# An adaLN transformer block on one core: feed-forward units of 1, 1, 2, 4, 4, 4 tiles, feature-major first keys, and a new order of loads and instructions

## The chip, the core and the metric

The kernel runs on one core of a Trainium2 chip. A core has engines that run side by side, each with its own in-order queue: TensorE (PE in the profile, its weight loads PEld), VectorE (DVE), ScalarE (ACT), GpSimd (POOL) and SyncE (SP), which here issues nearly all DMA transfers. Matmuls write to PSUM, which the kernel divides into a double bank for the attention sums (`kv_ps`) and six single banks (`one_ps`). The metric is the device time of one execution in microseconds (us), the median over runs.

## What is computed

One block with adaptive layer norm, over S = 2048 tokens of width D = 512, all in bf16:

```python
mod = (silu(c) @ w_mod)           # sa, ca, ga, sb, cb, gb: six rows of 512
h = layernorm(x) * (1 + ca) + sa
x = x + ga * A(h)
h = layernorm(x) * (1 + cb) + sb
x = x + gb * B(h)
```

```python
# A: linear attention, 32 heads of 16
q, k, v = h @ wqkv
pq, pk = q @ w_phi, k @ w_phi     # one 16 x 16 matrix per head
phi = [softmax(p), softmax(-p)]   # over 16 features, for q and for k
o = (phi_q @ (phi_k^T v)) / (phi_q @ sum(phi_k) + 1e-6)
return o @ wo
# B: feed-forward, F = 1376
return (silu(h @ w_gate) * (h @ w_up)) @ w_down
```

## The kernel before, in words

Tokens are cut into 16 tiles of 128, four tiles to a chunk (`x_ch`, 512 tokens each). Every step of the block is written as an operation of a planner (`pl.op`) with the buffers that it reads and writes, its estimated cost, and sometimes a choice of engines. `ORDER` (lines 46 to 87) is a long list, written out by hand or by a search, of operation numbers and engine choices. `Plan.run` walks through it, gives each operation a start time from its cost table, hands out the slots of the rotating buffers, and emits all operations by that start time. What each engine executes, and in which sequence, is thus fixed at build time; on the chip semaphores only make it wait. Where the planned start times leave PE idle, `fill` (line 1012) puts in matmuls on a tile of ones (line 1029), whose result is never used.

The work has these stages.

1. Loads (lines 428 to 438), all on SP's queue in order of their planned times: `x` of chunk 0, `wk`, `wphi`, the first third of `w_mod` in two pieces, `x` of chunk 1 in two pieces with `wq` between, `wv`, `x` of chunks 2 and 3. Later weights are queued further on.
2. Modulation columns. `silu(c)` (lines 445 to 457), then `mod_cols` (line 462): matmuls of the `w_mod` columns with it (line 468), copied out as `modA` (shift and 1 + scale) by two DVE instructions.
3. Folding. `w_phi` is spread into a block-diagonal matrix `BD` (lines 489 to 500). `fold_phi` (line 504) multiplies it into `wk` and `wq`: turn the weight (on PE for `wk`, by DMA transpose for `wq`), copy it out (`WT`, line 519), multiply by `BD` (line 526), write it back over the weight (line 529). So `pk = h @ Wk2` takes one matmul chain.
4. First norm (`first_norm`): `bn_stats` per tile on DVE (line 345), `rstd`, then the normalized tile `xn`. `turn_tile` (line 553) turns the first four tiles on PE into one bank each, and ACT or DVE evacuate it in two halves as `hT`, feature-major, with the modulation applied (lines 565 and 567). Later tiles go through `modulate_T` or a DMA transpose.
5. Keys and values (`k_tile`, line 615): four matmuls of 512 columns for `pk` (line 622), two exps on ACT into `e` (line 633), four matmuls for `v` (line 626), sums over 16 features on DVE (`S`, line 639), reciprocals, the weighted `va` (line 649), POOL's multiply (line 656). `kv_tile` adds a tile's `phi_k^T [v, 1]` into `kv_ps` (line 662). When all 16 are in, DVE masks the sum into `KVZ` (lines 771, 773).
6. Queries (`q_tile`): the same with `wq` into a tile `eq` of its own for each of the 16 tiles, `Sq` on DVE (line 693), then a DMA transpose into `pT` (line 704).
7. Attention of a tile (`attend_tile`): eight matmuls (line 805), a reciprocal `A`, the division into `o` (line 809). `turn` turns `o` into `oT`, on PE for the first two tiles and by DMA on SP (line 828) after that. `project` multiplies by `wo` (line 838), adds to `x` on DVE (line 841), and does the second norm. `second_T` turns that and applies `modB`.
8. Feed-forward in units of `UNITS` (line 33): `(chunk, first tile, tiles)`. `prepare` does stage 7 for the tiles of a unit, one or two at a time. `ffn_tail` does the last 96 of the 1376 hidden features, `ffn_gu` (line 878) the others in groups that fill a bank of 512: with w tiles, 4 / w blocks of 128 features, so that one matmul has 128 w columns (line 890). ACT takes silu of the gate bank (line 897); the product with the up bank is made by DVE (line 900), or for every other group by ACT's copy and POOL (lines 904, 906). `ffn_down` (line 946) accumulates 11 matmuls of 512 columns for each tile (line 962), scales, adds and stores (line 982).

Of the kernel before, what the change touches and what calls it, by code (L numbers as in the profile page):

```python
# [7 lines left out]
BF16 = mybir.dt.bfloat16  # L8
FP32 = mybir.dt.float32
ACT = mybir.ActivationFunctionType  # L10
ALU = mybir.AluOpType
# [21 lines left out]
UNITS = [(0, 0, 1), (0, 1, 1), (0, 2, 1), (0, 3, 1), (1, 0, 2), (1, 2, 2), (2, 0, 2), (2, 2, 2), (3, 0, 2), (3, 2, 2)]  # L33


def fm_size(m):
# [10 lines left out]
    0, 4, 8, 44, 64, 48, 52, 132, 116, 12, 56, 68, 76, 72, 172, 80, 164, 136, 176, 16, 60, 148, 100, 120, 168, 196, 200, 124, 85, 152, 180, 140,  # L47
    156, 88, 105, 92, 184, 108, 204, 190, 208, 128, 98, 216, 20, 240, 161, 228, 212, 264, 144, 225, 194, 112, 220, 420, 272, 244, 268, 32, 276, 24,
    28, 233, 248, 312, 36, 252, 236, 257, 376, 548, 281, 364, 512, 424, 284, 260, 428, 320, 432, 40, 294, 400, 552, 516, 324, 316, 588, 290, 480,
    592, 329, 296, 304, 472, 301, 380, 332, 524, 308, 596, 437, 338, 388, 520, 384, 444, 368, 372, 464, 456, 484, 440, 416, 529, 852, 556, 342, 404,  # L50
    476, 756, 448, 452, 532, 460, 856, 392, 408, 584, 468, 560, 344, 544, 488, 492, 510, 536, 396, 800, 760, 764, 502, 498, 541, 412, 600, 565, 572,
    1064, 506, 628, 1068, 808, 816, 1072, 624, 932, 768, 568, 605, 608, 984, 724, 632, 988, 820, 576, 636, 358, 860, 928, 350, 361, 792, 692, 732,
    354, 728, 773, 892, 804, 956, 1312, 812, 580, 796, 960, 824, 700, 848, 964, 1316, 612, 780, 896, 620, 828, 616, 864, 776, 784, 845, 788, 869,
    640, 968, 833, 972, 992, 888, 842, 938, 1000, 1280, 952, 976, 996, 946, 949, 904, 900, 876, 660, 1004, 942, 909, 872, 980, 838, 1160, 884, 881,
    916, 1276, 912, 1240, 920, 696, 1009, 1164, 1244, 736, 1324, 1028, 1168, 1016, 1304, 924, 1172, 1021, 1196, 1012, 1200, 1328, 1024, 740, 1294,
    1177, 644, 1252, 744, 1184, 1336, 1289, 1236, 1180, 1076, 1208, 1297, 1248, 648, 1257, 1264, 1189, 1204, 1332, 1341, 1286, 1492, 1496, 1192,
    1212, 748, 664, 1269, 1217, 1320, 1260, 1344, 1532, 1348, 1272, 1572, 1500, 1612, 1576, 1504, 1396, 1356, 1224, 1300, 1220, 1584, 1080, 652,
    1536, 1232, 1540, 1509, 1229, 1360, 668, 656, 1589, 1544, 1516, 1616, 1512, 1352, 1549, 1528, 1521, 1568, 1580, 1524, 1624, 1556, 1620, 1596,
    1592, 1629, 1561, 1601, 1604, 1636, 1641, 1552, 1608, 1084, 1564, 1632, 1128, 1136, 1716, 1644, 1648, 1796, 1800, 1780, 704, 1804, 1088, 1808,
    1652, 1748, 1724, 672, 1828, 1784, 1788, 1832, 1836, 1132, 1720, 752, 1792, 1404, 1400, 1408, 1756, 1308, 1684, 1032, 1092, 1840, 1660, 1844,  # L60
    2288, 2292, 1428, 1848, 708, 2296, 2300, 1036, 676, 1040, 1852, 1856, 2452, 1688, 712, 1860, 716, 720, 1752, 680, 1044, 1096, 684, 1864, 1436,
    1432, 1460, 1104, 1692, 1656, 1364, 1869, 2456, 2304, 1872, 1100, 1048, 1880, 1052, 2460, 2136, 2308, 1877, 1884, 1948, 688, 1056, 2312, 2140,
    1944, 1368, 1468, 1060, 1464, 2316, 1924, 1372, 2144, 1108, 1412, 1928, 1888, 1112, 1908, 2440, 1936, 1912, 2320, 1916, 1140, 2444, 2326, 1116,
    1120, 2148, 2152, 1416, 2328, 1144, 2448, 1892, 1932, 1920, 1984, 1124, 1940, 1952, 1148, 1896, 2338, 2156, 1988, 2334, 1960, 1900, 1964, 2160,
    2164, 1152, 1992, 2345, 2168, 1956, 1376, 2464, 1472, 2341, 2400, 2348, 2404, 1996, 2174, 2692, 1904, 1156, 2352, 2408, 2176, 2696, 1420, 1380,
    1384, 1476, 2384, 2700, 2000, 1388, 2392, 2492, 2496, 2181, 1968, 2356, 2004, 1480, 2704, 2468, 2193, 2190, 1424, 2364, 2008, 2186, 2380, 2412,
    2248, 2012, 2708, 2368, 2372, 1392, 2016, 2388, 2472, 2500, 2712, 2020, 2360, 2396, 2025, 1972, 2216, 2256, 2036, 2040, 2028, 2956, 2716, 2196,
    2376, 2476, 1484, 2960, 2504, 2252, 1488, 2964, 2228, 2508, 2032, 2236, 2260, 2480, 2484, 2513, 2490, 2516, 2044, 2048, 2944, 1440, 2096, 2416,
    2100, 2948, 1444, 1448, 1452, 1664, 2200, 2420, 1668, 1672, 1676, 2104, 2424, 2744, 2052, 2720, 2952, 1456, 3208, 2108, 2748, 2204, 2533, 2752,
    2232, 2525, 2530, 2724, 2756, 2212, 2968, 2240, 1680, 2522, 3212, 2760, 2728, 3216, 2076, 2220, 2732, 2736, 2536, 2742, 2540, 1696, 2224, 3196,  # L70
    2208, 2608, 2765, 1700, 2084, 3200, 1760, 2996, 2972, 2616, 2428, 3204, 1704, 1708, 1764, 2244, 2544, 2060, 1728, 2768, 1768, 2548, 2064, 3448,
    2080, 2068, 1772, 2782, 1712, 2773, 2556, 2778, 2576, 3220, 1732, 2785, 3000, 3452, 1776, 2976, 1736, 3456, 2628, 2788, 2792, 2088, 1740, 1744,
    3460, 2072, 2980, 2984, 2264, 2092, 3004, 2584, 3464, 3248, 2988, 3008, 3468, 2993, 3224, 2268, 3252, 3012, 3228, 3712, 3472, 3716, 3017, 2636,
    2272, 3232, 3236, 2612, 2796, 3720, 2560, 3256, 3240, 2800, 3020, 3260, 3700, 3264, 2564, 3704, 1976, 2056, 2112, 3476, 3708, 3480, 2620, 3026,
    3500, 2632, 3245, 3504, 3508, 3724, 3033, 3037, 2116, 3030, 2624, 3040, 2276, 3512, 3516, 3044, 2120, 3269, 3484, 3272, 3132, 2592, 2640, 2572,
    3488, 3492, 3521, 3498, 2568, 2124, 3752, 2596, 2600, 3140, 2552, 3756, 2580, 2804, 3285, 3278, 1980, 3760, 3524, 2588, 2604, 3728, 1824, 3281,
    3289, 3732, 2280, 3048, 3292, 3736, 3296, 3300, 3537, 3764, 2668, 3530, 3542, 2672, 3740, 3768, 3533, 3744, 2676, 2828, 3544, 3304, 3749, 3052,
    2836, 3548, 3774, 3776, 2680, 2685, 2644, 2648, 2880, 2888, 2652, 2884, 2848, 2656, 2892, 2688, 3790, 3782, 3056, 2844, 3785, 2824, 2864, 3793,
    2852, 3796, 2432, 2436, 2832, 2808, 2128, 2856, 3800, 2816, 2812, 2820, 2860, 3816, 3804, 2840, 2920, 3808, 2896, 2132, 2872, 3308, 2868, 2876,
    2900, 2904, 3824, 2924, 2928, 3820, 2932, 2908, 3832, 3836, 3840, 3828, 3844, 3076, 3552, 2937, 3080, 3084, 3136, 3848, 3088, 2940, 3928, 3092,  # L80
    3852, 3144, 3860, 3872, 3812, 3868, 3876, 3096, 3856, 3100, 3864, 3880, 3884, 3060, 1812, 2284, 2660, 3932, 3104, 3888, 3896, 3064, 3556, 3892,
    3116, 3108, 3068, 3124, 2912, 3112, 3120, 3072, 3900, 3936, 3128, 3172, 3312, 3148, 3176, 3180, 3184, 3152, 3320, 3156, 3904, 2916, 3316, 3908,
    3332, 3912, 3940, 3945, 3948, 3328, 3189, 3324, 2664, 3340, 3560, 3336, 3916, 3364, 3368, 3921, 3384, 1817, 3160, 3372, 3344, 3376, 3380, 3392,
    3348, 3352, 3388, 3356, 3360, 1821, 3400, 3404, 3396, 3408, 3424, 3192, 3428, 3432, 3616, 3436, 3600, 3441, 3624, 3924, 3564, 3620, 3165, 3584,
    3444, 3636, 3628, 3592, 3168, 3580, 3568, 3412, 3640, 3572, 3588, 3632, 3576, 3416, 3644, 3608, 3596, 3604, 3648, 3676, 3612, 3652, 3680, 3420,
    3684, 3656, 3688, 3660, 3952, 3664, 3692, 3956, 3696, 3960, 3669, 3964, 3672, 3968,
# [35 lines left out]
class Plan:  # L122


    HOP = {"PE": 0.24, "DVE": 0.2, "ACT": 0.2, "POOL": 0.14, "SP": 0.0, "XBAR": 0.08, "NONE": 0.0}
    OWN = {"PE": 0.0, "DVE": 0.19, "ACT": 0.19, "POOL": 0.12, "SP": 0.0, "XBAR": 0.0, "NONE": 0.0}
    DMA = (1.7, 385e3, 0.5, 0.7, 1.3, 1.0)
# [81 lines left out]
def kernel(  # L209
# [23 lines left out]
    wts = ctx.enter_context(tc.tile_pool(name="wts", bufs=1))  # L233
    attn = ctx.enter_context(tc.tile_pool(name="attn", bufs=1))
    lnp = ctx.enter_context(tc.tile_pool(name="lnp", bufs=1))
    ps = ctx.enter_context(tc.tile_pool(name="ps", bufs=1, space=PSUM))

    slots = {"raw": 2, "st6": 6, "one": 6, "four": 1, "xn": 4, "raw1": 2, "nmr": 4, "ln2": 6, "xn2": 2, "WT": 2, "e": 6, "S": 3, "R": 3,
             "va": 6, "Sq": 4, "Rq": 4, "pT": 4, "A": 2, "o": 2, "oT": 2, "sg": 3, "gu": 13, "gul": 3, "sgl": 3,
             "usb": 2, "ot": 3, "fg": 3}  # L240
    pl = Plan(slots)
    pools = {}

    fixed = {}

# [185 lines left out]
    for k in (0, 2):  # L431
        later(wmod_sb[:, k:k + 2, 0:2 * D], wmod_v[:, k:k + 2, 0:2 * D], bm1[k:k + 2], 512)
# [636 lines left out]
```

The softmax here doesn't subtract the row's maximum and nothing guards it: scores larger than these inputs give would overflow.

## Time and profile before

| | us |
|---|---|
| median of 3 runs | 201.79 |
| span of the profiled execution, first to last instruction | 200.1 |
| PE busy (matmuls x1743) | 192.4 (96%) |
| PE weight loads busy (x1765) | 131.7 (66%) |
| DVE busy | 136.7 (68%) |
| ACT busy | 111.4 (56%) |
| POOL busy | 124.4 (62%) |
| share of the chain that ended last on PE | 85% |
| gate and up matmuls (line 890, x800), busy | 75.4 |
| down matmuls (line 962, x167 and 11 of the last half tile), busy | 39.6 and 1.4 |
| DMA moved | 24.22 MB, mean 121 GB/s |

How to read it: the span is one execution under the profiler; the median is taken over runs that include what lies around the span. The page's slices cut the span into 40 pieces of 5 us and give tenths of busy time. A table of stages gives the busy microseconds of each engine and the number of its instructions. The chain of waits goes back from the last instruction to what released it each time, so that its pieces lie one after the other in time. In the timeline, an instruction is followed by the idle time before it and what ended that. Matmul records overlap, since one starts before the one ahead has drained; the time from start to start is what one more matmul costs.

### The profile page before, as it was taken

To read this page: it belongs to the slowest core of one execution; us is meant where nothing else is said; L and a number is where in the kernel's file an instruction comes from. 1 tells how busy PE (TensorE), PEld (TensorE's weight loads), DVE (VectorE), ACT (ScalarE), POOL (GpSimd) and SP (SyncE) were. 2 spreads that over 40 slices of the span, in tenths; PEclk is the share of its full clock that TensorE was granted. 3 is DMA by queue.
4 is the path that set the end of the run, shared out by engine and by line. 5 is a ranking of instruction groups with operands and counts; after the bars stand their busy time and mean duration, and the time that the engine had idled before them with its cause. 6 is when DMAs were issued, how large, how long until landed. Compare 5 with 4: busy or idle time off the path is not lost.

```text
span 200.1 us, 4635 instructions
## 1 busy us (share of the span) xinstructions
PE 192.4 (96%) x1743; PEld 131.7 (66%) x1765; DVE 136.7 (68%) x274; ACT 111.4 (56%) x249; POOL 124.4 (62%) x209
## 2 busy tenths in 40 slices
PE   7898999999999989999999999999999999999993
PEld 2654546454554867896796676688488865867852
DVE  5898999999899989998997896432041404434143
ACT  2689999989779963572554717344154230421510
POOL 3445999999998697687896689744123920210602
PEclk9999999999999999999999999999999999999999
DMA  6998998991963694956695463042010001101102
GB/s 212 342 316 193 278 244 238 227 358 25 216 209 76 131 130 95 114 108 124 113 194 105 64 131 79 3 92 66 3 56 10 5 26 52 52 3 41 36 6 66
DMA packets 51081, 24.22 MB, mean 121 GB/s; under 512 B 42257, under 2 KB 47858, under 8 KB 51058
## 3 DMA queue, kind: packets, MB, share of 16 engines
q1 hardware_dynamic: 50912, 23.85, 50.8%
q8 instruction: 14, 0.23, 0.5%
q14 instruction: 9, 0.07, 0.1%
q10 hardware_dynamic: 146, 0.07, 0.1%
HBM read 11.58 MB, written 2.10 MB: 68 GB/s over the span
## 4 chain that ended last, share of the span: by engine, by line
PE 85%; ACT 5%; DVE 5%; DMA 2%; issue 1%; DVEq 0%; SPq 0%; ACTq 0%
PE one_ps L890 33%; PE one_ps L962 19%; PE one_ps L626 7%; PE one_ps L838 6%; PE one_ps L685 5%; PE one_ps L622 5%; PE one_ps L930 3%; DVE st L345 2%; PE kv_ps L662 2%; DMA oT<-o 2%; ACT e L633 2%; PE kv_ps L805 2%; ACT hT L565 1%; ACT eq L689 1%; PE kv_ps L1029 1%
## 5 line engine op out<-in xcount | busy, mean ns | idle before, releaser
L890 PE MATMUL one_ps<-hT,wgu_sb 128*128 128x256 bf16 (+1 forms) x800 | 75.4, 251 | 0.0
L890 PEld LDWEIGHTS <-wgu_sb 128*128 128x128 bf16 x800 | 65.3, 98 | 9.4
L906 POOL TENSOR_TENSOR gu<-usb,sg 128x512 bf16<-128x512 bf16 x16 | 18.5, 1157 | 38.1 <-ACT usb L904 18.8
L897 ACT ACTIVATE sg<-one_ps 128x512 bf16<-128x512 f32 (+1 forms) x42 | 23.5, 576 | 32.1 <-PE one_ps L890 27.8
L962 PE MATMUL one_ps<-wd_sb,gu 128*128 128x512 bf16 (+3 forms) x167 | 39.6, 372 | 0.5
L900 DVE TENSOR_TENSOR gu<-one_ps,sg 128x512 bf16<-128x512 f32 (+1 forms) x26 | 16.6, 643 | 24.4 <-PE one_ps L890 20.2
L962 PEld LDWEIGHTS <-gu 128*128 128x128 bf16 (+1 forms) x187 | 17.9, 98 | 15.9
L973 DVE TENSOR_TENSOR fg<-one_ps,gab 128x512 bf16<-128x512 f32 (+1 forms) x16 | 10.5, 668 | 24.2 <-PE one_ps L962 23.4
L345 DVE BATCH_NORM_STATS2 st<-x_c 128x6 f32<-128x512 bf16 x32 | 21.3, 676 | 0.1
L639 DVE TENSOR_REDUCE S<-e 128x64 f32<-128x1024 bf16 x16 | 19.2, 1203 | 0.7 <-issue 0.5
L693 DVE TENSOR_REDUCE Sq<-eq 128x64 f32<-128x1024 bf16 x16 | 19.0, 1192 | 0.0
L700 POOL TENSOR_TENSOR eq<-eq,Rq 128x512 bf16<-128x512 bf16 x16 | 16.9, 1056 | 0.8
L689 ACT ACTIVATE eq<-one_ps 128x512 bf16<-128x512 f32 x32 | 17.1, 613 | 0.4 <-PE one_ps L685 0.3
L633 ACT ACTIVATE e<-one_ps 128x512 bf16<-128x512 f32 x32 | 16.8, 605 | 0.8 <-PE one_ps L622 0.6
L904 ACT CAST usb<-one_ps 128x512 bf16<-128x512 f32 x16 | 9.3, 583 | 14.2 <-PE one_ps L890 13.0
L656 POOL TENSOR_TENSOR e<-e,S 128x512 bf16<-128x512 bf16 x16 | 16.8, 1057 | 0.3
L626 PE MATMUL one_ps<-wv,hT 128*128 128x512 bf16 x61 | 15.7, 378 | 0.8 <-ACT e L633 0.6
L838 PE MATMUL one_ps<-wo_sb,oT 128*128 128x512 bf16 x60 | 15.6, 379 | 0.9 <-DMA oT<-o 0.7
L622 PE MATMUL one_ps<-wk,hT 128*128 128x512 bf16 x62 | 15.7, 379 | 0.1
L685 PE MATMUL one_ps<-wq,hT 128*128 128x512 bf16 x61 | 15.1, 379 | 0.1
L841 DVE TENSOR_TENSOR x_c<-x_c,one_ps 128x512 bf16<-128x512 bf16 x16 | 10.8, 674 | 6.0 <-PE one_ps L838 6.0
L393 ACT ACTIVATE xn<-x_c,ln_nmr,ln_rstd 128x512 bf16<-128x512 bf16 x10 | 8.1, 809 | 9.7 <-POOL ln_nmr L359 9.7
(112 smaller groups left out, 268.2 us busy)
## 6 DMA issues: line engine op xcount, KB each, us to landing
wmod_sb<-in_w_mod_dram SPq DMA_DIRECT2D x2, 1024.0 KB, 7.0
out_dram<-ot SPq DMA_DIRECT2D x15, 128.0 KB, 1.9
x_c<-in_A_x_dram SPq DMA_DIRECT2D x3, 512.0 KB, 4.1
wgu_sb<-in_B_w_gate_dram SPq DMA_DIRECT2D x1, 1376.0 KB, 6.8
wgu_sb<-in_B_w_up_dram SPq DMA_DIRECT2D x1, 1376.0 KB, 6.7
wd_sb<-in_B_w_down_dram SPq DMA_DIRECT2D x1, 1280.0 KB, 7.4
wmod_sb<-in_w_mod_dram SPq DMA_DIRECT2D x2, 512.0 KB, 6.4
wk<-in_A_wqkv_dram SPq DMA_DIRECT2D x1, 512.0 KB, 4.7
```

Source lines behind the costliest of these rows:

```text
L345: pl.op("DVE", r=reads, w=[st6], us=0.6, fn=lambda: nc.vector.bn_stats(st6()[:], src))
L622: nc.tensor.matmul(pk()[:], lhsT=hT[c_i][k][:, cols], rhs=Wk2[:, k, :], start=(k == 0), stop=(k == KD - 1))
L626: nc.tensor.matmul(v()[:], lhsT=hT[c_i][k][:, cols], rhs=wv_sb[:, k, :], start=(k == 0), stop=(k == KD - 1))
L633: nc.scalar.activation(e()[:, :, sg].rearrange("p g h f -> p g (h f)"), pk()[:].rearrange("p (g n) -> p g n", g=G), ACT.Exp, scale=(1.0, - ...
L639: pl.op("DVE", r=[e], w=[Ss], us=1.14, fn=lambda: nc.vector.tensor_reduce(Ss()[:].rearrange("p g s h -> p (g s h)"), e()[:].rearrange("p g ...
L685: nc.tensor.matmul(pq()[:], lhsT=hT[c_i][k][:, cols], rhs=Wq2[:, k, :], start=(k == 0), stop=(k == KD - 1))
L689: pl.op("ACT", r=[pq, btab], w=[be[sg]], us=0.48, fn=lambda sg=sg: nc.scalar.activation(eq[:, :, sg].rearrange("p g h f -> p g (h f)"), pq ...
L693: pl.op("DVE", r=be, w=[Sq], us=1.14, fn=lambda: nc.vector.tensor_reduce(Sq()[:].rearrange("p g s h -> p (g s h)"), eq[:].rearrange("p g s ...
L838: nc.tensor.matmul(a()[:], lhsT=oT()[:, j0 + j, :], rhs=wo_sb[:, j, :], start=(j == 0), stop=(j == KD - 1))
L890: nc.tensor.matmul(ps_()[0:fsz, q * n:(q + 1) * n], lhsT=wgu_sb[:, k, i, m * P:m * P + fsz], rhs=h2[k], start=(k == 0), stop=(k == KD - 1))
L897: pl.op("ACT", r=[g, btab], w=[sg], us=0.08 + 0.41 * L / CW, fn=lambda: nc.scalar.activation(sg()[0:fsz, 0:L], g()[0:fsz, 0:L], ACT.Silu))
L962: nc.tensor.matmul(fp()[:], lhsT=b()[0:fsz, c0:c0 + P], rhs=wd_[0:fsz, m, wcs], start=(m == 0), stop=(m == FM - 1))
```

## The change

Six things change together.

- `UNITS` becomes one unit of one tile, another, one of two, and three of four, instead of four of one tile and six of two. A unit of four still prepares two tiles at a time. `ffn_tail` works on two tiles at a time in a buffer of its own (`gut`), and `gu` has 20 slots instead of 13.
- The keys of tiles 0 and 1 no longer wait for the folded weight: `first_keys` multiplies the plain `wk` with `hT` of both tiles, 256 columns wide, into feature-major keys `kT`, and `k_tile` multiplies those by `BD`. `kT` lies in the memory of the last tile's `eq`. Folding `wk` goes on as before, now after these reads.
- `turn_tile` turns each half of a tile into a bank of its own.
- `mod_cols` lets a one-row matmul write the zeros and ones first, so that one copy takes out `modA` or `modB`.
- The first loads are cut and listed anew.
- The planner's costs are changed throughout, and `ORDER` is a new list.

Only costs, that is estimates of the planner, change in the places that are not shown.

```diff
-UNITS = [(0, 0, 1), (0, 1, 1), (0, 2, 1), (0, 3, 1), (1, 0, 2), (1, 2, 2), (2, 0, 2), (2, 2, 2), (3, 0, 2), (3, 2, 2)]
+UNITS = [(0, 0, 1), (0, 1, 1), (0, 2, 2), (1, 0, 4), (2, 0, 4), (3, 0, 4)]
...
-             "va": 6, "Sq": 4, "Rq": 4, "pT": 4, "A": 2, "o": 2, "oT": 2, "sg": 3, "gu": 13, "gul": 3, "sgl": 3,
+             "va": 6, "Sq": 4, "Rq": 4, "pT": 4, "A": 2, "o": 2, "oT": 2, "sg": 3, "gu": 20, "gut": 5, "gul": 3, "sgl": 3,
...
-    later(x_ch[0][:], x_v[0], bx[0:4], 512)
-    later(Wk2[:], wqkv_v[:, :, D:2 * D], bwk[0:1], 560)
-    later(wphi_sb[:], A_w_phi.rearrange("h (q t) f -> (h q) (t f)", t=4), [bphi], 80)
-    for k in (0, 2):
-        later(wmod_sb[:, k:k + 2, 0:2 * D], wmod_v[:, k:k + 2, 0:2 * D], bm1[k:k + 2], 512)
-    later(x_ch[1][:, 0:2, :], x_v[1][:, 0:2, :], bx[4:6], 256)
-    later(x_ch[1][:, 2:4, :], x_v[1][:, 2:4, :], bx[6:8], 256)
+    later(x_ch[0][:, 0:2, :], x_v[0][:, 0:2, :], bx[0:2], 230)
+    for k, n, kb in ((0, 2, 660), (2, 1, 300), (3, 1, 300)):
+        later(wmod_sb[:, k:k + n, 0:2 * D], wmod_v[:, k:k + n, 0:2 * D], bm1[k:k + n], kb)
+    later(Wk2[:], wqkv_v[:, :, D:2 * D], bwk, 560)
+    later(wphi_sb[:], A_w_phi.rearrange("h (q t) f -> (h q) (t f)", t=4), [bphi], 100)
+    later(x_ch[0][:, 2:4, :], x_v[0][:, 2:4, :], bx[2:4], 270)
+    for t in (0, 2):
+        later(x_ch[1][:, t:t + 2, :], x_v[1][:, t:t + 2, :], bx[TPC + t:TPC + t + 2], 270)
...
         def fm(k):
+            if k == 0:
+                nc.tensor.matmul(mp()[:, 0:8], lhsT=ones[0:1, 0:P], rhs=zero_one[0:1, :], start=True, stop=False, skip_group_check=True)
...
         def fc():
-            nc.vector.tensor_copy(mt[:, 0:KD], mp()[:, 0:KD])
-            nc.vector.tensor_scalar_add(mt[:, KD:2 * KD], mp()[:, KD:2 * KD], 1.0)
+            nc.vector.tensor_copy(mt[:], mp()[:])
...
     def turn_tile(xn, parts, q, t):
-        tp = bank("T", [P, KD, P], BF16)
...
         for jp in range(2):
+            tp = bank("T", [P, 2, P], BF16)
+
+            def ft(jp=jp, tp=tp):
+                for jj in range(2):
+                    j = 2 * jp + jj
+                    nc.tensor.transpose(tp()[:, jj, :], xn()[:, q, j * P:(j + 1) * P], ident_b[:])
...
+    kT = eqs[NT - 1][:].rearrange("p g s h f -> p (g s h f)").rearrange("p (j m) -> p j m", j=KD)
+    bkT = [Buf(), Buf()]
+
+    def first_keys():
+        for jp in range(2):
+            pp = bank("kv", (P, 2, 2 * P))
+
+            def f(k, jp=jp, pp=pp):
+                for jj in range(2):
+                    j = 2 * jp + jj
+                    nc.tensor.matmul(pp()[:, jj, :], lhsT=Wk2[:, k, j * P:(j + 1) * P], rhs=hT[0][k][:, 0:2 * P],
+                                     start=(k == 0 and jj == 0), stop=(k == KD - 1), skip_group_check=True)
+            for k0 in (0, 2):
+                pl.op("PE", r=[bhT[0][t][k] for t in (0, 1) for k in (k0, k0 + 1)] + bwk[k0:k0 + 2], w=[pp], us=0.44,
+                      fn=lambda f=f, k0=k0: (f(k0), f(k0 + 1)))
+            pl.op([("ACT", 0.48, lambda jp=jp, pp=pp: nc.scalar.copy(kT[:, 2 * jp:2 * jp + 2, :], pp()[:])),
+                   ("DVE", 0.6, lambda jp=jp, pp=pp: nc.vector.tensor_copy(kT[:, 2 * jp:2 * jp + 2, :], pp()[:]))],
+                  r=[pp], w=[bkT[jp]])
...
+        def fk2():
+            for j in range(KD):
+                nc.tensor.matmul(pk()[:, j * P:(j + 1) * P], lhsT=kT[:, j, cols], rhs=BD[:, j].rearrange("p h f -> p (h f)"),
+                                 start=True, stop=True)
...
-        pl.op("PE", r=h_bufs(i) + bWk2, w=[pk], us=0.865, fn=fk)
+        if i < 2:
+            pl.op("PE", r=bkT + [bBD], w=[pk], us=0.23, fn=fk2)
+        else:
+            pl.op("PE", r=h_bufs(i) + bWk2, w=[pk], us=0.865, fn=fk)
...
     first_norm(0, 2)
+    bmodA = mod_cols(modA, 0, [[b] for b in bm1])
+    first_T(0, 2)
+    first_keys()
     fold_phi(D, Wk2, bWk2, bwk)
     first_norm(2, 2)
-    bmodA = mod_cols(modA, 0, [[b] for b in bm1])
-    first_T(0, 2)
...
     def ffn_tail(unit, guT):
...
+        g = min(w, 2)
+        guT[FM - 1] = []
+        for p0 in range(0, w, g):
+            gu = sb("qf", "gut", [P, 2 * P], BF16)
+            ps_ = bank("gu")
```

In the built program, SP issues the first transfers in this sequence: `x` of chunk 0 in two halves, `x` of chunk 1 in two halves, `w_mod` in three pieces, `wphi`, `wk`, `x` of chunk 2, `wv`, `wq`. PE does the first key matmuls between the turns of `wk`, and none of the filler matmuls stands after them (before, five stood between the last `kv_tile` and the second norm of tile 0). DVE has the eight `bn_stats` of chunks 0 and 1 ahead of its copy of `modA`.

## The prediction

> **What bounds the kernel now.** I read the 40 slices first, then the busy time by stage, then the chain of waits, then the timeline of the start and of 57 to 74 us.
>
> ```profile
> PE   7898999999999989999999999999999999999993
> DVE  5898999999899989998997896432041404434143
> ```
>
> TensorE (PE) is busy from the second slice to the last, VectorE (DVE) up to the 24th. By stage (us, then busy us of PE, weight loads, DVE, ACT, POOL):
>
> ```profile
> 0.00:11.70 11.70, 9.61 (x112) 5.66 (x114) 8.19 (x28) 6.21 (x14) 4.82 (x18) 1.00 0.87 292
> 11.70:18.00 6.30, 5.71 (x40) 3.06 (x39) 6.15 (x18) 5.67 (x14) 3.40 (x6) 1.00 1.09 231
> 18.00:57.30 39.30, 38.93 (x324) 20.86 (x330) 38.11 (x61) 36.80 (x102) 37.16 (x62) 1.00 0.87 233
> 120.00:197.00 77.00, 76.61 (x578) 56.53 (x582) 26.19 (x48) 26.35 (x49) 29.89 (x34) 1.00 0.12 34
> ```
>
> From 18 to 57 us all four engines are full; after 120 us PE alone. Busy time flatters PE, so I count necessary work: matmuls in the program times the start-to-start time that the chain shows.
>
> ```profile
> 48.56 0.86 PE one_ps L685 x4
> ...
> 81.76 4.02 PE one_ps L890 x72
> ...
> 182.29 8.74 PE one_ps L890 x80
> ```
>
> 512 columns take 0.216 us (four in 0.86), 256 take 0.109 (8.74 / 80), 128 take 0.056 (4.02 / 72). So 429 x 0.216 + 502 x 0.109 + 408 x 0.056 + 64 of 192 columns x 0.083 + 256 of 68 columns x 0.031 + 84 small x 0.025 = 185.4 us without the fillers of line 1029. What PE lacks is clock time minus necessary work issued: 8.0 us at the first keys (11.72 us, 3.7 done), 9.0 at 18 us, 9.3 at the first attention matmul (57.30), 10.2 at the first gate/up (66.56), 11.3 at the first down (73.78), 11.4 at PE's end (196.83). Behind that lie 3.3 us of last add and store. So the time is 185.4 + 11.4 + 3.3 = 200.1, and only the 9.0 of the start and the 2.4 gained between 18 and 74 us can shrink. Of the 2.4 the largest is this:
>
> ```profile
> 68.31 3.96 DMA oT<-o
> 72.32 0.39 PE one_ps L838
> ```
>
> The transpose of o is issued late (SP stood behind three pT transposes from 62.51) and the projection waits for it.
>
> **What the Trainium skill says.** "TensorE: Matmul & The Clock Gate", Back-to-back issue gap: columns / 2.4 + 2.5 ns, so larger matmuls save only the 2.5. The trace agrees (216, 109, 56 ns). "Perfetto Trace Analysis", Identifying the Most-Contended Engine: judge TensorE by weight-load share. Here that is 66% and 98 ns per load, yet starts keep column pace even at 256 columns, so I give nothing for fewer loads. Same page, Matmuls: groups should rotate through banks so evacuation overlaps; the trace agrees, ACT's hT waits 0.6 for DVE's hT on a shared bank. "PSUM — Partial Sum Buffer", Engine vs sequencer instructions: ACT and DVE queues are strict first-in-first-out; the start's working rests on it.
>
> **The change, part by part.**
>
> *Units.* 160 matmuls of 128 and 400 of 256 columns go, 240 of 512 come: 160 x 0.056 + 400 x 0.109 = 52.6 against 51.8, **-0.8**. Evacuations stay 512 wide; three up halves move from DVE to ACT and POOL (3 x 0.58, 3 x 1.16), hidden after 120 us, where each is busy a third. SP issues three transposes fewer. The two zero_one matmuls cost 0.05 of PE, under waits for wmod; one modA instruction less saves 0.1 of DVE, in the start below. Were that cover gone, each would count in full, a tenth of a microsecond.
>
> *Keys from unfolded weights.* Eight 512-column matmuls go (1.73), 16 of 256 (1.75) and 8 of 128 (0.45) come: **+0.5**. The 256-column form with hT moving is not in the trace; I take the gate/up row of that width (0.109), between 0.107 (columns alone) and 0.126 (two of 128 columns and a start each). ACT gets two copies of kT (0.98). kT lies in the tile eq15, whose own exp comes some 40 us later: no wait. PE's work is 185.1 in all.
>
> *First loads.* Landings before: wk 5.88 (issue 1.18 + 4.7), the wmod halves 8.09 and 9.55, wq 11.68 (3.68 + 8.0), wv 13.89 (4.79 + 9.1). So 512 KB take 1.46, and the small w_phi 0.75 (8.09 - 5.88 - 1.46). In the built program SP's order is x 0 and x 1 in four halves, wmod in three, w_phi, wk, x 2, wv, wq: landings 3.7, 4.4, 5.15, 5.9; 7.3, 8.1, 8.8; 9.55; 11.0; 12.5; 13.9; 15.4. The key weights come 5 us later, x 1 over 4 us earlier, wv as before. The ninth load waits for the first to land, long before its turn. Queued behind on SP are x 3 and the four wq transposes: they slip from 11.8 to about 16, and the first fold of wq, at 16.8 before, is placed after 14.6 us of PE work, about 24: no wait.
>
> *The start, by queues.* DVE gets x at 3.75; eight bn_stats (0.595 each), aggregates (0.09) and the silu steps (0.65) all stand before its modA copy: 9.9 (10.14 before). Then ACT evacuates hT at 0.70 a pair: the first two end 11.4, and the first key matmul starts there, with 2.4 us of work done: 9.0 lacking, against 8.0. ACT goes on in order: hT 12.1, two WT copies (0.48) 13.0, hT 13.7, kT 14.2 and 14.7, wk 15.2, 15.7, 16.15. PE meanwhile does 16 key matmuls, weight turns and folds, v of one tile (wv 13.9), and the two BD products when banks come free (16.0, 16.6: the second after DVE's wk copy, which stands behind four bn_stats of x 2). The first exp starts about 16.4 against 13.99, tile 2's keys at 16.8 with 7.2 done: 9.6 lacking against 9.0: **+0.6**. What is queued behind the second BD product on PE, tile 2's keys, needs the same copy, so that wait is paid once. Bounds: -0.5 (PE without a gap from wk's landing: 11.0 with 1.9 done lacks 9.1, and 8.5 if the loads land 0.6 sooner) and +1.6 (ACT's hT pairs at the 0.81 of a lone pair and another bank late). From there banks (73, 75, 74) come free just as PE asks.
>
> *18 to 74 us.* DVE's work up to KVZ grows by 1.8 (one Sq 1.13, one WT copy 0.36, two hT 0.58, less small ones) but its idle time falls from 4.85 (by stages up to KVZ, 55.81) to about 2.3, as x comes early: KVZ at 55.1, PE there at 56.3. No wait. After that the built order does more projections before the first gate/up (58.0 of work done, 56.3 before), so tile 0's chain has 6 us instead of 4.6, and no filler stands after the first keys (five did at 55 to 66, 0.85 us). The oT for the next two projections: o done 63, one pT ahead on SP, +3.2 to landing: 66.3, PE at 66.6. I take 0.75 of waits in place of 2.4 (0.2 at the first turn, which stands behind an Sq on DVE; 0.35 up to KVZ as before; 0.2 for the projections): **-1.65**. What is late next would be VectorE. Bounds: 0 and 4 (rivals 1 and 2).
>
> *End.* Same last add and store: 3.3.
>
> Sum: -0.3 + 0.6 - 1.65 = -1.35 from the span of 200.1; runs lie 1.7 above the span (median 201.79), so **200.4**.
>
> **The rivals.**
> 1. *No wait after 18 us:* the order leaves no room. PE lacks 9.6 at the end: -0.3 - 1.8 = 199.7; with the start 0.5 better than by my queues (the exact landing of x decides), 199.2. For it: after 74 us the kernel before loses 0.1. Against: 18 to 57 us is full on four engines.
> 2. *VectorE late, slower:* DVE becomes the bound. If its idle before KVZ is 1.2 above my 2.3 (e's come 2.4 later from ACT), attention waits us for us; the u halves and projections that DVE must free hold up to six banks at 75 to 90 us, since two more Sq's, one more o and one more x + A stand before the first gate/up multiply. Idle as before (4.85) gives KVZ 57.6, 1.4 late; the same again in the banks: 200.4 + 2.8 = 203.2. Against: 23 to 24 slices of DVE at 8 to 9 left PE no gap before.
> 3. *The oT wait stays:* SP's pT waits for POOL's eq as at 62.51 (5.18 for three); 1.1 comes back: 201.5. And the change doesn't do what it says: keys start no earlier by my working, which is already in the sum.
>
> **How the numbers follow.** Forecast 0.52 (199.6 to 201.2), rival 1 0.22, rival 2 0.16, rival 3 0.10. The range drops the outer parts of rivals 1 and 2: 198.6 to 203.3. Two per cent, about what a measurement of this kernel can tell from no change, is 197.75 and 205.8. Below needs PE to lack 7.7, when wk alone lands at 11.0 with 2 us done: only if loads run faster than 512 KB in 1.2, 0.1. Above needs rival 2 doubled: 0.09.
>
> **What would show it.** Right: first key matmul near 11.4, first exp near 16.4, KVZ near 55, gate/up 216 ns apart, weight loads near 50%, PE ending near 195.5. Wrong: keys before 10.5 (landings), DVE idle over 4 us before KVZ, or ACT and DVE groups waiting on banks between 75 and 120 us.

## The result, and the profile after

The changed kernel takes 202.12 us (median of 7, 201.56 to 205.57) against 201.69 for the kernel before on the same chip: ratio 1.0027, interval 1.0010 to 1.0043. It is 0.4 us longer, not 1.4 shorter. The profiled execution has a span of 200.1 us, the same as before. Some executions of the changed kernel lose about 2 us, a few more than 3, to a granted clock that falls to half (for 3.4 us in the profiles that show it); where I give a mean span below, it is over executions with a granted clock of 0.997 or more (here 200.1 in 6 of 7; 199.8 for the kernel before, taken beside the experiments), and the ratios leave the longest executions out.

The slices and the busy times of the profiled execution:

```profile
PE 193.4 (97%) x1463; PEld 108.3 (54%) x1463; DVE 141.1 (70%) x285; ACT 107.6 (54%) x242; POOL 123.7 (62%) x202
...
PE   7699999999999999999999999999999999999993
...
DVE  6899999998999999979997946446405202314443
```

The weight loads fell from 66% to 54% as forecast, and PE looks full. Two rows of the table of stages (us, then busy us of PE, weight loads, DVE, ACT, POOL) show where it is not:

```profile
0.00:11.70 11.70, 8.65 (x88) 4.46 (x89) 8.87 (x35) 5.42 (x11) 4.25 (x18) 1.00 0.83 283
...
118.00:137.00 19.00, 18.44 (x95) 8.42 (x93) 10.46 (x22) 9.85 (x18) 10.66 (x17) 1.00 0.27 54
```

PE was busy 9.61 us of the first stage before; in the second row, a stretch for which the prediction has no term, 0.56 us is missing. What PE lacks, counted as in the prediction (clock time minus necessary work issued) but from start to start for both kernels, is:

| PE lacks, us | before | after |
|---|---|---|
| at the first key matmul | 7.9 (11.72) | 9.7 (12.18) |
| at tile 2's keys (before: 18 us) | 8.9 | 9.7 (17.04) |
| at the first attention matmul | 9.1 (57.30) | 10.1 (57.08) |
| at the first gate/up | 10.0 (66.56) | 10.3 (68.46) |
| at the first down | 11.1 (73.78) | 10.3 (76.58) |
| at PE's end | 11.2 (196.83) | 11.4 (196.82) |

Read down, the kernel before loses 2.2 between 18 and 74 us and 0.15 after that. The changed kernel loses 0.6 up to its first down matmul, and then 1.1. The gain of the middle is there, and 0.95 of it is given back later. The timeline of PE at that place (start, us, engine, line, tiles, count, idle time before):

```profile
127.59 1.03 PE L926 MATMUL one_ps<-hT,wgu_sb 128*128 128x512 bf16 x4
128.90 3.63 PE L926 MATMUL one_ps<-hT,wgu_sb 128*128 128x512 bf16 x16 [0.28 <-DVE hT L895]
...
133.56 1.89 PE L926 MATMUL one_ps<-hT,wgu_sb 128*128 128x512 bf16 x8
135.73 1.02 PE L926 MATMUL one_ps<-hT,wgu_sb 128*128 128x512 bf16 x4 [0.28 <-DVE x_c L877]
```

Four starts at 0.216 from 127.59 end at 128.45, eight from 133.56 at 135.29: PE stands twice for 0.44 us (the 0.28 is less because a matmul's recorded end lies behind the moment at which the next could start). These two waits are 0.88 of the 0.95. The chain of waits tells what it stood for:

```profile
122.28 4.64 DMA raw<-xn
...
126.95 0.35 DVE hT L895
...
127.45 0.57 DVE o L845
128.03 0.83 DVE hT L895
...
130.09 2.22 POOL gu L942 x2
...
133.38 0.28 POOL ln_nmr L362
...
133.68 1.40 DVE xn L392
135.08 0.60 DVE x_c L877
```

A turned tile of the second norm (`raw`) lands after 4.64 us where an undisturbed one takes 3.1. Behind it DVE makes one half of `hT`, then the division `o`, which nobody waits for soon, and only then the half that PE wants. The next norm follows late on POOL, where two products `gu` (2.22) stand among its steps, and the second wait is again DVE's queue: `xn` (1.40) stands before the add `x_c` that frees PE's bank. The DMA view for 121 to 126.5 us (queue, kind, packets, MB, share of 16 engines; then tiles, queue, us to landing):

```profile
q1 hardware_dynamic: 1216, 0.30, 28.1%
q8 instruction: 1, 0.02, 1.3%
...
raw<-xn SPq DMA_TRANSPOSE x1, 4.6
gut<-gul SPq DMA_TRANSPOSE x1, 3.6
```

One instruction fetch (the queue of kind instruction; 16 KB, at 124.94) fell into the transposition in flight. A late landing alone does not stop PE: the `raw` transposition issued at 89.85 took 4.61 us, again with a fetch in it, and PE has no wait behind it.

### The profile page after: what moved, and what is told of

It is laid out like the page before. It is cut to its first block, busy times and chain, and to the rows that moved or that the text cites. A ratio compares the mean times of both kernels' runs of the same rounds, so it can differ in the third digit from the quotient of the medians.

```text
span 200.1 us, 4021 instructions
## 1 busy us (share of the span) xinstructions
PE 193.4 (97%) x1463; PEld 108.3 (54%) x1463; DVE 141.1 (70%) x285; ACT 107.6 (54%) x242; POOL 123.7 (62%) x202
## 4 chain that ended last, share of the span: by engine, by line
PE 86%; DMA 5%; POOL 2%; DVE 2%; ACT 1%; SPq 1%; issue 0%; DVEq 0%
PE one_ps L926 30%; PE one_ps L1004 18%; PE one_ps L720 7%; PE one_ps L659 7%; PE one_ps L874 6%; PE one_ps L655 6%; DMA wmod_sb<-in_w_mod_dram 3%; PE one_ps L972 2%; DMA raw<-xn 2%; PE kv_ps L698 2%; PE kv_ps L841 2%; POOL gu L942 1%; PE one_ps L531 1%; PE one_ps L634 1%; PE one_ps L474 1%; PE one_ps L752 1%
## 5 line engine op out<-in xcount | busy, mean ns | idle before, releaser
L926 PE MATMUL one_ps<-hT,wgu_sb 128*128 128x512 bf16 (+2 forms) x480 | 76.3, 308 | 0.6 <-DVE hT L895 0.3
L926 PEld LDWEIGHTS <-wgu_sb 128*128 128x128 bf16 x480 | 40.2, 98 | 29.4 <-DVE hT L895 0.8
L942 POOL TENSOR_TENSOR gu<-usb,sg 128x512 bf16<-128x512 bf16 x19 | 22.2, 1171 | 28.8 <-ACT usb L940 15.4
L1004 PE MATMUL one_ps<-wd_sb,gu 128*128 128x512 bf16 (+1 forms) x160 | 38.5, 372 | 0.0
L936 DVE TENSOR_TENSOR gu<-one_ps,sg 128x512 bf16<-128x512 f32 (+1 forms) x22 | 14.4, 661 | 21.3 <-PE one_ps L926 13.3
L1004 PEld LDWEIGHTS <-gu 128*128 128x128 bf16 x170 | 16.3, 98 | 16.1
L1015 DVE TENSOR_TENSOR fg<-one_ps,gab 128x512 bf16<-128x512 f32 (+1 forms) x16 | 10.6, 668 | 12.8 <-PE one_ps L1004 12.7
L940 ACT CAST usb<-one_ps 128x512 bf16<-128x512 f32 x19 | 11.2, 587 | 15.1 <-PE one_ps L926 11.8
L1019 POOL TENSOR_TENSOR ot<-x_c,fg 128x512 bf16<-128x512 bf16 x9 | 10.3, 1154 | 9.6 <-DVE fg L1015 5.3
L735 POOL TENSOR_TENSOR eq<-eq,Rq 128x512 bf16<-128x512 bf16 x15 | 15.9, 1061 | 0.5
L655 PE MATMUL one_ps<-wk,hT 128*128 128x512 bf16 x56 | 13.2, 379 | 0.0
```

The lines of the kernel that those rows point to most:

```text
L655: nc.tensor.matmul(pk()[:], lhsT=hT[c_i][k][:, cols], rhs=Wk2[:, k, :], start=(k == 0), stop=(k == KD - 1))
L926: nc.tensor.matmul(ps_()[0:fsz, q * n:(q + 1) * n], lhsT=wgu_sb[:, k, i, m * P:m * P + fsz], rhs=h2[k], start=(k == 0), stop=(k == KD - 1))
L942: pl.op("POOL", r=[usb, sg], w=[gu], us=0.17 + 0.98 * L / CW, fn=lambda: nc.gpsimd.tensor_tensor(gu()[0:fsz, 0:L], usb()[0:fsz, 0:L], sg() ...
L1004: nc.tensor.matmul(fp()[:], lhsT=b()[0:fsz, c0:c0 + P], rhs=wd_[0:fsz, m, wcs], start=(m == 0), stop=(m == FM - 1))
```

## The experiments

Three questions: what makes the late waits, what sets the start, and whether the parts costed at nothing cost nothing.

**after_again**, the changed kernel once more, unaltered.

> The changed kernel once more, unaltered, beside the two below. If its two TensorE waits after 120 us belong to its order and not to one execution, they are there again: a wait at the first gate and up matmuls of the third unit of four (near 128 us) when the transposition of xn issued near 122 us takes 4.6 us, and another near 135 us. Lack at TensorE's end 11.2 to 11.5, ratio to the kernel before 1.001 to 1.004.

Measured: 203.83 (8 executions), ratio 1.0095 (1.0064 to 1.0126); six of eight have a clock of 0.990 to 0.992 and a mean span of 202.0, two have full clock and 200.1. The `raw` transposition takes 4.62 again, and the wait at 128.66 is back with 0.42; the second did not show. So the first wait comes back in another execution of the same program, the second need not, and the fall of the clock varies from execution to execution.

**a_late**: DVE's queue in two places, nothing else.

```diff
+        sooner = {780: 126.0, 901: 132.13}
...
-        for o in sorted(self.ops, key=lambda o: (o.start, o.n)):
+        for o in sorted(self.ops, key=lambda o: (sooner.get(o.n, o.start), o.n)):
```

The second half of `hT` goes ahead of `o`, the add ahead of `xn`.

> Two instructions change places on VectorE: a piece of hT (L895) goes ahead of the division o (L845) at about 127 us, and the addition to x (L877) goes ahead of a normalization (L392) at about 133 us. Theory 'queue order': the changed kernel's two TensorE waits after 120 us (0.44 us each at 128.2 and 135.1) come from what stood ahead on VectorE; both go, TensorE's lack at its end falls from 11.4 to about 10.5, and the time falls by 0.9 us (ratio to the kernel before about 0.998, to the changed kernel's 1.0027). Rival 'units of four': a matmul of 512 columns needs the last pair of its four tiles in any case, so the wait comes back within the next 10 us; the time falls by 0.3 us or less.

Measured: profiled span 199.3, mean span at full clock 199.5 (12 of 22 executions) against 200.1; ratio 0.9997 (0.9974 to 1.0021). The transposition is as late as before (4.66), and PE no longer stands:

```profile
127.65 4.48 PE L927 MATMUL one_ps<-hT,wgu_sb 128*128 128x512 bf16 x20
...
133.16 2.75 PE L927 MATMUL one_ps<-hT,wgu_sb 128*128 128x512 bf16 x12
```

Twenty matmuls start without a gap where four and sixteen stood apart. PE's end lacks 10.6, 0.85 less. The rival, that units of four hold up PE in any queue order, falls: they are all still there.

**i_fetch**: the first filler matmuls cut into narrow ones, so that PE's instructions, and with them the fetches, come at other times.

```diff
+            wide = 64 if t0 < 7.0 else CW
-            while left >= 128:
-                fns.append(lambda n=min(left, CW): f(n))
-                left -= CW
+            while left >= min(128, wide):
+                fns.append(lambda n=min(left, wide): f(n))
+                left -= wide
```

> The changed kernel with its filler matmuls before 7 us made of 64 columns instead of 512, the same columns in all: 97 more matmuls and weight loads at the start of TensorE's program, nothing else. In the traces a 16 KB fetch of instructions (the DMA queue of kind instruction, about one for each 250 of TensorE's) falls on a transposition in flight, and that one lands after 4.2 to 5.3 us in place of 3.1 (in the changed kernel at 69.3, 92.5, 105.7 and 124.9 us). Theory 'fetch': 194 more instructions move the fetches by three quarters of their distance; the transposition of xn issued near 122 us lands after 3.1 us, the waits near 128 and 135 us go, lack at TensorE's end 10.4 to 10.7, the time 0.8 us below after_again. Rival 'order': which transposition is slow doesn't depend on it, the one near 122 us takes 4.6 us again and both waits stay.

Measured: profiled span 199.6, mean span at full clock 199.7 (10 of 22), ratio 1.0030 (1.0007 to 1.0053), in which some falls of the clock still count. The DMA view for 122 to 126 us:

```profile
q1 hardware_dynamic: 1216, 0.30, 37.8%
...
raw<-xn SPq DMA_TRANSPOSE x1, 3.1
gut<-gul SPq DMA_TRANSPOSE x1, 2.4
```

The same 1216 packets and no fetch: the two transpositions take 3.1 and 2.4 instead of 4.6 and 3.6. The waits at 128 and 135 us are gone with DVE's queue as in the changed kernel, as PE's timeline shows (one record of the first block is missing; its twenty starts fill the time up to the next line):

```profile
127.98 4.48 PE L926 MATMUL one_ps<-hT,wgu_sb 128*128 128x512 bf16 x19
...
133.49 2.75 PE L926 MATMUL one_ps<-hT,wgu_sb 128*128 128x512 bf16 x12
```

Both links are shown now: without the fetch, or without the queue behind it, no wait. The other profiles agree. With DVE's queue unaltered and a fetch 2.5 to 2.7 us after the issue of this transposition the first wait is there (0.42 to 0.53 us in the changed kernel, after_again, c_folded and f_nox1b); where the transposition takes 3.0 to 3.6 (i_fetch, j_both, d_split, g_warm) it is not.

**d_split**: each 512-wide gate/up matmul as two of 256, the weights loaded twice.

```diff
-                for k in range(KD):
-                    nc.tensor.matmul(ps_()[0:fsz, q * n:(q + 1) * n], ... rhs=h2[k],
+                for c0 in range(0, n, 2 * P):
+                    c1 = min(n, c0 + 2 * P)
+                    for k in range(KD):
+                        nc.tensor.matmul(ps_()[0:fsz, q * n + c0:q * n + c1], ... rhs=h2[k][:, c0:c1],
```

> Each gate and up matmul of 512 columns (240 of them) is made as two of 256 with the weights loaded twice; all else as in the changed kernel. Theory 'columns alone': 480 x 0.109 in place of 240 x 0.216 is 0.5 us of work; the time is 0.3 to 0.6 us longer than the changed kernel's. Rival 'weight loads count': 240 more loads of 98 ns show at least in part, more than 2 us longer.

Measured: ratio 1.0015 (0.9992 to 1.0038), mean span at full clock 199.9 (8 of 12).

```profile
PE 196.2 (97%) x1703; PEld 133.0 (66%) x1703; DVE 142.3 (70%) x285; ACT 107.7 (53%) x242; POOL 123.2 (61%) x202
```

```profile
130.41 4.53 PE L928 MATMUL one_ps<-hT,wgu_sb 128*128 128x256 bf16 x40
```

The first line is the page's, the second PE's timeline. Loads are back at 66%, and over all the 480 narrow matmuls the starts are 0.109 us apart: at that pace the loads cost nothing, as the prediction had it, and the rival's 2 us are not there. The 480 added PE instructions moved the fetch to 119.42; that `raw` transposition took 4.2, the next one 3.0, and PE has no wait where the changed kernel waits: 40 starts run through. So the total cannot settle a few tenths: it holds the 0.5 us that the extra starts cost and lacks the 0.9 of the late waits.

**c_folded**: the keys of tiles 0 and 1 from the folded weight, as before; in `ORDER` one operation moves by two places.

```diff
-                pl.op("PE", r=[bhT[0][t][k] for t in (0, 1) for k in (k0, k0 + 1)] + bwk[k0:k0 + 2], w=[pp], us=0.44, ...
+                pl.op("PE", us=0.0, fn=lambda: None)
-            pl.op([("ACT", 0.48, ...
+            pl.op("ACT", us=0.0, fn=lambda: None)
...
-        if i < 2:
-            pl.op("PE", r=bkT + [bBD], w=[pk], us=0.23, fn=fk2)
-        else:
-            pl.op("PE", r=h_bufs(i) + bWk2, w=[pk], us=0.865, fn=fk)
+        pl.op("PE", r=h_bufs(i) + bWk2, w=[pk], us=0.865, fn=fk)
```

> Keys of tiles 0 and 1 from the folded weight, as in the kernel before; loads, units and the order of everything else as in the changed kernel. 2.2 us of matmuls go (24 of L634 and L650), 1.7 us come back. Theory 'late weights': with the key weights landing at 11.1 us the fold is what TensorE would wait for, so the feature-major keys buy what the load order costs: the first folded key matmul comes at about 17.5 us, the lack after the start is about 11.7 us against 9.7, and the time is 1.5 us longer than the changed kernel's. Rival 'VectorE and ScalarE set the start anyway': lack about 10.2, time within 0.3 us of the changed kernel.

Measured: 204.57 (4), ratio 1.0145 (1.0097 to 1.0192); the two executions at full clock have spans of 201.9 and 202.1, 1.9 above the changed kernel's. With `wk` landing behind 2 MB of `x` and `w_mod`, and in an order of instructions made for them, the unfolded keys are thus worth 1.9 us, by two executions; unfolded keys and new loads together leave the start 0.8 worse than before. Its profiled execution also shows the clock fall. By stages (the last three numbers: granted clock, DMA share, GB/s):

```profile
8.00:11.00 3.00, 1.57 (x33) 1.24 (x33) 2.48 (x6) 1.09 (x2) 0.77 (x1) 1.00 1.06 379
11.00:14.50 3.50, 3.50 (x44) 2.65 (x43) 2.18 (x10) 2.31 (x6) 1.89 (x4) 0.53 0.96 337
```

PE was busy 1.57 of 3.0 us, waiting for `w_mod`; from 11.18 to 14.59 the clock is at half (0.50 by the same view of that stretch).

**f_nox1b**: the second half of `x` of chunk 1 (tiles 6 and 7) isn't loaded; its place is set to zero.

```diff
+        if t == 0:
             later(x_ch[1][:, t:t + 2, :], x_v[1][:, t:t + 2, :], bx[TPC + t:TPC + t + 2], 270)
+        else:
+            pl.op("XBAR", w=bx[TPC + t:TPC + t + 2], us=0.5, kb=270, fn=lambda: nc.gpsimd.memset(x_ch[1][:, 2:4, :], 0.0))
```

> The second half of x of chunk 1 (256 KB) is not loaded: tiles 6 and 7 are zeros. Every later transfer has 256 KB less ahead of it. Theory 'landings set the start': the w_mod pieces land 0.7 to 1.5 us sooner, the copy of modA at about 9.4, the first key matmul at about 11.3, lack after the start about 8.9 in place of 9.7, and the time falls by 0.8 us. Rival 'the queues of VectorE and ScalarE set the start': the first key matmul may come sooner, but tile 2's keys stay at 16.8 to 17.0 and the time falls by 0.2 us or less.

Measured: ratio 1.0001 (0.9980 to 1.0023), mean span at full clock 199.7 (10 of 12), 0.4 shorter. Its profiled execution had late landings (`w_mod` at 10.54) and the clock fall, so it says nothing on the start. 0.4 lies between what the two theories expect: inconclusive by itself.

**g_warm**: eight more filler matmuls of 512 columns before the wait for `w_mod`, so that PE is not idle there.

```diff
-            left = int((o.start - t0) * (1200 if t0 < 7.0 else 2400))
+            left = int((o.start - t0) * (1200 if t0 < 7.0 else 2400)) + (8 * CW if o.n == 27 else 0)
```

> The changed kernel with eight more filler matmuls of 512 columns ahead of the first w_mod matmul, where TensorE stood idle for 1.6 us. Theory 'idle array': the idle time there lets the granted clock fall to half for 3.4 us in some executions (it did from 10.4 to 13.8, 11.1 to 14.5 and 11.2 to 14.6 us in three of the profiles so far); with the gap filled the clock stays full from the first rise on, and the executions spread less. Rival: the late transfers alone make those executions long; the spread stays. Both: where the clock is full anyway nothing changes, ratio to the changed kernel within 0.2%.

Measured: full clock in 6 of 6, but 203.18, ratio 1.0089 (1.0064 to 1.0114). With the gap filled the clock holds. The time went elsewhere; the DMA view for 25.5 to 27 us, and PE's timeline:

```profile
q8 instruction: 1, 0.02, 6.7%
...
raw<-xn SPq DMA_TRANSPOSE x1, 5.3
```

```profile
32.07 0.39 PE L655 MATMUL one_ps<-wk,hT 128*128 128x512 bf16 x1
33.57 0.60 PE L655 MATMUL one_ps<-wk,hT 128*128 128x512 bf16 x2 [1.11 <-POOL hT L599]
```

Sixteen more PE instructions at the start (a matmul and a load for each filler) put a fetch, at 26.03, into another transposition, which takes 3.7 in the changed kernel, and the keys wait 1.28 us for that tile.

**h_both**: a_late and g_warm together.

> The two exchanges on VectorE of the run a_late and the eight fillers of g_warm together. Theory 'queue order': 0.9 us shorter than g_warm (no wait near 128 and 135 us, lack at the end about 10.5), ratio to the kernel before about 0.998. Rival 'units of four' (the wait comes back) or 'one execution' (the waits are no regular part of the changed kernel): less than 0.3 us shorter.

Measured: 203.49 (6), full clock in all, ratio 1.0092 (1.0066 to 1.0117). It is not 0.9 shorter than g_warm: the wait of 1.28 is there (33.27), the `raw` issued at 124.99 takes 3.5 here (3.6 in g_warm, where PE has no late wait either), so there was none left to remove, and the copy of `modA` comes 1.58 us after `w_mod`'s last landing instead of 0.6, behind the fillers.

**j_both, k_all, l_short**: i_fetch with 15 fillers of 256 columns before the wait; that with a_late's queue; that with fillers of 128 columns.

```diff
+            if o.n == 27:
+                fns += [lambda: f(2 * P)] * 15
```

> As i_fetch, and 15 more fillers of 256 columns ahead of the first w_mod matmul, so that TensorE doesn't stand idle there (224 more instructions than the changed kernel). Theory 'fetch' and 'idle array' together: granted clock 0.997 or more in every execution, no wait near 32 us as in g_warm and h_both (whose 16 more instructions put a fetch on the transposition issued near 25 us), none near 128 and 135 us; spans of 199.0 to 199.6, ratio to the kernel before 0.995 to 0.999. Rival: fillers ahead of the first w_mod matmul cost what they save, spans of 200.5 to 201.5 as in g_warm.

> As j_both, with the two exchanges on VectorE of a_late. If the fetch no longer falls on the transposition near 122 us, the exchanges have nothing to save: within 0.2 us of j_both. If it still does, 0.8 us shorter than j_both.

> As k_all, with the 15 fillers ahead of the first w_mod matmul 128 columns wide instead of 256. In k_all and j_both the copy of modA came 0.9 and 1.4 us after the last w_mod piece landed, against 0.6 in the changed kernel: the fillers ran too long. Theory: with half the columns the copy comes 0.6 to 0.7 us after the landing again, the granted clock stays at 0.997 or more in nearly all executions, no wait near 128 and 135 us, and spans are 199.1 to 199.7: ratio to the kernel before 0.996 to 1.000. Rival: the array stands idle long enough again for the clock to fall in some executions, spans of 200.5 to 202 among them.

Measured: 202.18, 202.05 and 202.06; ratios 1.0028 (1.0009 to 1.0046), 1.0011 (0.9988 to 1.0034), 1.0026 (1.0009 to 1.0043). The clock holds in 20 of 22, 14 of 14 and 14 of 14 executions. In time nothing is won: in j_both and k_all the copy of `modA` follows `w_mod`'s landing by 1.35 and 0.94 us, so the fillers run over their wait. In l_short it follows by 0.67, but in that execution `w_mod` itself lands at 10.54. None of these beats the kernel before, and so the expected spans of 199.0 to 199.7 did not come: mean spans are 200.2, 200.1 and 200.3.

**e_nofill**: the kernel before with its fillers ending at 50 us instead of 90.

```diff
-FILL_FROM, FILL_TO, FILL = 1.3, 90.0, 0.85
+FILL_FROM, FILL_TO, FILL = 1.3, 50.0, 0.85
```

> The kernel before without the fillers after 50 us (five matmuls, 0.85 us). Theory: they fill time in which TensorE would wait for tile 0's projection and norm, so nothing is gained: the waits show as idle time near 55 and 65 us, and the time is within 0.2 us of the kernel before. Rival: the fillers themselves hold up the work behind them, and part of the 2.4 us that the kernel before lost between 18 and 74 us was theirs: 0.4 to 0.9 us shorter.

Measured: ratio 1.0003 (0.9990 to 1.0016). PE's timeline shows in their place open waits:

```profile
65.04 0.40 PE L411 MATMUL one_ps<-ident_b,xn 128*128 128x128 bf16 x4 [0.29 <-ACT xn L393]
...
65.94 3.95 PE L890 MATMUL one_ps<-hT,wgu_sb 128*128 128x128 bf16 x64 [0.18 <-ACT hT L419]
...
71.78 1.04 PE L838 MATMUL one_ps<-wo_sb,oT 128*128 128x512 bf16 x3 [0.73 <-DMA oT<-o]
```

The first two lay under fillers; the third, for the transposed `o`, was open in the kernel before too. The fillers lay on waits, so their absence after the change is no gain of its own.

## Why the prediction was wrong

| term of the sum, us | forecast | measured |
|---|---|---|
| PE's work | -0.3 | -0.2 |
| start | +0.6 | +0.8 |
| 18 to 74 us | -1.65 | -1.6 |
| after the first down matmul | 0 | +0.95 |
| last add and store | 0 | 0 |
| span | -1.35 | 0 |
| outside the span | 1.7 | 1.93 |

**The step that failed** is the term for PE's waits behind the first down matmul, which the sum put at nothing: it carried the 1.65 of the middle unchanged to PE's end. The one reason that the forecast gives is in *Units*: the work added to other engines is "hidden after 120 us, where each is busy a third". A busy share of a third said that DVE, ACT and POOL had time on average; it did not say that the one instruction PE waits for stands first in its queue. In its place the profile shows 0.95 us: one landing 1.5 us late cost 0.44 + 0.44, because `o` and later `xn` stood on DVE ahead of what PE wanted, and moving two DVE instructions (a_late) or the fetch (i_fetch) takes both waits away. The answer was rival 2's kind (an engine's queue late), at 128 us instead of 75 to 90, and of 0.95 instead of 2.8.

That the fetch falls just there is chance, as far as the argument goes: nothing in the prediction placed the fetches. Whether the kernel before would have borne such a landing is not shown; in its profile no `raw` transposition after 80 us takes more than 3.5. In e_nofill, with the same units of one and two, one took 4.31 at 108.94 and PE did not wait.

**PE's work.** 512-wide gate/up starts are 216 ns apart, loads count nothing (d_split): right, 0.1 off. (The prediction's products add up to 185.6, not 185.4, so the kernel before lacks 11.2 at PE's end, as in the table above, and not 11.4; the forecast difference hardly changes.) The Trainium skill ("TensorE: Matmul & The Clock Gate", Back-to-back issue gap) gives the prediction's columns / 2.4 + 2.5 ns for a lone matmul, and about 131 ns at 512 columns for a stream of loads and matmuls; here the stream keeps 216.

**The start** came out near in size by luck, for another reason. The working had DVE's queue set `modA` at 9.9. The timeline of PE, then that of DVE, show:

```profile
8.34 0.55 PE L474 MATMUL one_ps<-silucT,wmod_sb 128*128 128x1 bf16 x16 [1.61 <-DMA wmod_sb<-in_w_mod_dram]
...
12.18 0.60 PE L634 MATMUL one_ps<-hT,wk 128*128 128x256 bf16 x4
```

```profile
8.72 0.68 DVE L348 BATCH_NORM_STATS2 st<-x_c 128x6 f32<-128x512 bf16 x1
10.30 0.17 DVE L479 COPY modA<-one_ps 128x8 f32<-128x8 f32 x1 [0.90 <-PE one_ps L474]
```

DVE was through its eight `bn_stats` at 9.4 and stood 0.90 us for PE, and PE for `w_mod`. From the second half of `x` of chunk 1 on, the loads ahead of `wk` landed 0.9 to 1.0 later than forecast (the last piece of `w_mod` at 9.68, not 8.8; `wk` at 11.14, not 11.0). In the profiled executions of the changed kernel, after_again, a_late, c_folded, d_split, g_warm, i_fetch and l_short that piece lands between 9.50 and 10.84, and the copy follows it by 0.59 to 0.68 us each time. First keys 12.18 (11.4), first exp 16.82 (16.4), tile 2's keys 17.04 (16.8). So the landing of `w_mod`, with `x` of both chunks ahead of it on the queue, sets the start: in the profiles at full clock (the changed kernel, after_again, a_late, g_warm, i_fetch, l_short) tile 2's keys come 7.3 to 7.4 us after it, whether it lands at 9.50 or at 10.54. In the changed kernel PE starts without a wait all through these 7.4 us, and 1.0 of them is filler matmuls; whether these still cover waits or hold up the keys was not tried.

**18 to 74 us** was right in its sum. KVZ at 55.61 (55.1), first attention 57.08 (56.3), and the wait for the transposed `o` is gone: 0.6 of waits where I took 0.75. That wait of the kernel before had a part I didn't see: its transposition, issued at 68.31, took 3.96 instead of 3.1, and a fetch, at 69.81, lies in it too.

**Outside the span** lie 1.93 us (mean of 7 executions) against 1.8 before; I had carried over one execution's 1.7. And the profile of the kernel before was 0.3 longer than its mean span. So equal profiled spans go with medians that differ by 0.4. Not in the sum at all is the fall of the clock, which costs about 2 us where it comes; the kernel before shows none in 134 executions beside the experiments.

Not settled: why the landings at the start differ by 1.3 us between these executions, and whether taking `x` of chunk 1 from ahead of `w_mod` wins the 0.8 back (f_nox1b can't tell; the loads in another order were not tried). Nor was it tried what the order, the earlier `x`, the bank for each half of a turned tile and the single copy of `modA` are worth each: the 1.6 of the middle belong to all of them together.

## What to carry to other kernels

Where PE is the bound, follow a gain in one stage to the end of the kernel: ask of each later wait which single instruction releases it and what stands ahead of that one in its queue, for a low busy share of the engine doesn't answer this. Order a shared queue by who is waited for, so that a late landing has slack. A small change to the number of instructions moves the instruction fetches, and so can give or take about a microsecond somewhere else (0.9 in the changed kernel, 1.3 in g_warm); look for that before explaining such a difference by the edit.

## What the runs showed of the hardware

**Instruction fetches disturb DMA transpositions.** The Trainium skill ("Runtime: NRT & Kernel Launch", Instruction fetch mechanics) says that a sequencer refills its memory in 16 KiB blocks of 256 instructions through DMA, at a cost that is mostly hidden. The counts agree: 14 fetches for 3508 matmuls and loads before, 11 for 2926 after, 13 for 3406 in d_split, one for 251 to 266. Hidden they are not where one falls into a transposition. After 100 us, over all the traces of this case, the 31 `raw` transpositions without a fetch take 3.04 to 3.24 us to landing; of ten with a fetch 1.0 to 3.0 us after their issue eight take 4.2 to 4.7, and two (in g_warm and h_both, with the fetch 2.6 and 3.0 after) 3.1; with a fetch 0.4 to 0.7 us after the issue, three take 3.5 to 3.6. In g_warm one goes from 3.7 to 5.3. That the fetches are PE's is inferred from the counts, and from their times moving with added PE instructions.

**The clock falls after a short idle time.** The same skill ("TensorE: Matmul & The Clock Gate", Part 1: The HAM clock gate) has half rate after at least one idle window of about 3.4 us. The length agrees: 11.18 to 14.59 is 3.41 us. The condition does not: in c_folded PE was busy 1.57 of the 3.0 us ahead, with no idle time in one piece above 1.5 us. What decides is not shown: in the changed kernel PE was busy 1.80 of the 3.41 us from 5.20 on, and the clock held. Filling the gap holds it (60 of 62 executions of g_warm, h_both, j_both, k_all and l_short, against 50 of 87 of the changed kernel and its other variants), and in after_again its loss costs 1.9 us.
